# V's blocks of keys 400 instead of 392 bytes apart in SBUF, in an attention kernel with a small expert layer

## The chip, the core and the metric

The kernel runs on one core of a Trainium2 chip. The core has a matrix engine (TensorE, "PE" in the profile; its weight loads are shown apart as "PEld"), VectorE ("DVE"), ScalarE ("ACT"), GpSimd ("POOL") and SyncE ("SP"), and 16 DMA engines. On-chip memory is SBUF, which all engines read, in 128 partitions, and PSUM, into which TensorE writes its products. The metric is the device time of one execution in microseconds (us); lower is better.

## What is computed

The input x is 2048 tokens x 640, in bf16. It is normalised by token (xn). Then two parts follow.

Part A is attention over a cache. There are 32 heads of width 192. The queries are xn @ wq; the keys and values are not computed but taken from a cache, of which only the last 512 keys of each head are used:

```python
q = (x @ wq) per head;  k, v = k_cache[:, :, Sk - 512:], v_cache[:, :, Sk - 512:]
p = softmax(q @ k.T * 192 ** -0.5)
s = concat_heads(p @ v) @ wo
```

Part B picks the two tokens with the highest score x @ w_r, runs a gated layer of width 1536 on them, weighs them with a sigmoid, and adds them to x at their places; a silu follows (g). The output is x + s * g.

## The kernel before

**Tiling.** Heads are worked in pairs: one head sits in partitions 0 to 63, the other in 64 to 127, so most matrix products are issued twice, once for each half r, and the two run side by side in the 64-row halves of TensorE. There are 8 groups of 4 heads (2 pairs a group), and for each group 4 stretches of 512 tokens. A *step* is a group, a stretch and a pair: 64 steps. A *block* b is half a step, 256 tokens: 128 blocks, each with two query tiles a of 128 tokens.

**Stages of a block.** The order on each engine is written out by hand: no scheduler moves anything (`manual_schedule`). From block 12 to 125 one pattern, `BLOCK = "A S0 M0 W m E0 B S1 M1 P E1 l"`, is followed; the blocks before and after have their own lists of tokens (`FIRST`, `LAST`).

- A, B (`q_phase`, L340): the queries of the next step, products with 512 or 256 columns; ScalarE copies them to SBUF (L352).
- S (`scores`, L367): queries times keys, 6 products with 512 columns for each query tile; PSUM has two buffers for them.
- M (`row_max`, L372): VectorE takes the row maxima.
- E (`exps`, L377): ScalarE takes the exponentials. When both tiles of a block are done, SyncE issues a transposing DMA (L383) that turns them into pT.
- P (`o_item`, for block b - 2): the products with V (`o_products`, L406), then the reciprocal of the row sums on VectorE (L413), the scaling into o_sb by VectorE for one head (L417) and by ScalarE for the other (L420), and a transposing DMA (L423) to oT.
- W (`w_item`, for item b - 6): the products with wo (L447), 24 with 320 columns, which VectorE adds to s_acc (L470). It uses the same PSUM banks as P, which must have been read out.
- m, l and the callbacks inside P: pieces of part B, loads for the next group, and the final sums.

**V in SBUF.** V's tile is `v_ring`, [128 partitions, 3 ring places, 8, VC] in bf16, a ring over pairs of heads. Key number 8e + k of a head lies in partition e (plus 64 for the second head) in block k, so k runs from 0 to 7 (`KB` = 8) and each partition holds 8 blocks of 192 values. `VC` is the distance of the blocks in elements. Element 192 of each block is set to 1.0 once at the start by GpSimd (L175); with it the product gives the row sum as its 193rd column. Elements from 193 on are never read or written.

A V load is issued by SyncE for each head (`v_piece`, L136), 32 in all; it writes 8 pieces of 384 bytes in each of 64 partitions. The products that read V are the 32 of a block in L406: for each tile a, for k from 0 to 7, for r in 0 and 1, 193 columns of `v_ring[half(r), ring place, k, 0:193]` move through the array against 128 columns of pT as weights.

v_ring is the last tile of the pool "big". The buffers of pools that are opened later (weights wq and wo, raw, ordered and transposed keys, queries, the first x tiles, part B's tiles) come after it in SBUF.

Of the kernel before, what the change touches and what calls it, by code (L numbers as in the profile page):

```python
# [21 lines left out]
def kernel(ctx, tc, A_x, A_k_cache, A_v_cache, A_wq, A_wo, B_x, B_w_r, B_w_gate, B_w_up, B_w_down, out):  # L22
# [5 lines left out]
    Dh = A_k_cache.shape[3]  # L28
# [49 lines left out]
    xnT = big.tile([P, NTB, DC, P], BF16, name="xnT")  # L78
    s_acc = big.tile([P, NTB, D], FP32, name="s_acc")

    RP, RO, RT, RV, VC = 3, 3, 7, 3, Dh + 4
    p_ring = big.tile([P, 2, 2, KB, 2, HK], BF16, name="pexp")
    pT_ring = big.tile([P, RP, 2, KB, P], BF16, name="pT")
    o_ring = big.tile([P, RO, CC, 2, HK], BF16, name="o_sb")
# [932 lines left out]
```

## Time and profile before

| | |
|---|---|
| median of 3 runs | 795.19 us (794.8 to 796.57) |
| the profiled execution | 796.98 us |
| its span, first to last instruction | 795.1 us |
| granted TensorE clock | 1.000 |
| busy: TensorE / VectorE / ScalarE / GpSimd | 98% / 75% / 66% / 39% |
| products of L406 (V) | 4096 |
| DMA: moved, mean rate | 141.77 MB, 178 GB/s |

Busy times are shares of the span. Matrix products overlap each other and their ends are modelled, so the time that one takes is better read from the starts of successive ones than from the length of one. "Idle before" in a group of instructions is time in which the engine stood still before them, with what ended it. The chain is followed back from the last instruction: at each step to what released it, or to the instruction ahead of it on its engine.

### The profile page before, as it was taken

What the parts mean: (1) busy time and instruction counts of PE and PEld (TensorE: products, weight loads), DVE (VectorE), ACT (ScalarE), POOL (GpSimd) and SP (SyncE); (2) the same over time, 40 slices, a digit from 0 to 9 for tenths busy, and PEclk for the clock granted to TensorE, in tenths of its full rate; (3) what the DMA queues carried; (4) which work ended last, traced back from release to release, by engine and by line L of the source; (5) the groups of instructions that cost most, each with busy time, mean ns of one, the idle gap of its engine ahead of it and who ended that gap; (6) DMA issues with size and microseconds to landing.
All of it is one profiled execution on the core that took longest, in us unless ns stands there. A gap on an engine that the chain in (4) does not pass through costs nothing.

```text
span 795.1 us, 26635 instructions
## 1 busy us (share of the span) xinstructions
PE 779.8 (98%) x11357; PEld 576.6 (73%) x11357; DVE 597.6 (75%) x1091; ACT 525.9 (66%) x952; POOL 313.8 (39%) x248
## 2 busy tenths in 40 slices
PE   8899999999999999999999999999999999999997
PEld 4457677777777677777777777777777777777775
DVE  7898788887778766767766777777777777766775
ACT  6676666666666666666666667767767776666662
POOL 1333111011110101001011499999996412565865
PEclk9999999999999999999999999999999999999999
DMA  9989999799999999999999999999999899999993
GB/s 238 191 174 167 160 192 172 134 195 168 179 204 184 179 196 200 191 181 215 182 213 158 180 189 185 149 163 180 163 188 160 148 188 178 200 174 177 177 176 87
DMA packets 443319, 141.77 MB, mean 178 GB/s; under 512 B 410436, under 2 KB 442696, under 8 KB 443200
## 3 DMA queue, kind: packets, MB, share of 16 engines
q1 hardware_dynamic: 433568, 130.83, 94.6%
q10 hardware_dynamic: 8672, 6.72, 3.5%
q0 software_dynamic: 960, 2.52, 1.2%
q8 instruction: 89, 1.46, 0.8%
q14 instruction: 30, 0.25, 0.1%
HBM read 39.98 MB, written 2.62 MB: 54 GB/s over the span
## 4 chain that ended last, share of the span: by engine, by line
PE 89%; DVE 5%; ACT 3%; DMA 2%; issue 1%; SPq 0%; DVEq 0%; ACTq 0%
PE w L447 25%; PE q_ps L340 23%; PE o_ps L406 20%; PE s L367 19%; DVE nm L372 1%; ACT pexp L377 1%; DMA pT<-pexp 1%; PE q_ps L309 1%; DMA v_sb<-in_A_v_cache_dram 1%; ACT o_sb L420 0%; DVE s_acc L470 0%; ACT xnT L283 0%; DMA x_in<-in_A_x_dram 0%; PE tp L282 0%; PE gu_ps L787 0%
## 5 line engine op out<-in xcount | busy, mean ns | idle before, releaser
L372 DVE TENSOR_REDUCE nm<-s 128x2 f32<-128x1024 f32 x256 | 312.9, 1223 | 120.0 <-PE s L367 114.6
L377 ACT ACTIVATE pexp<-s,nm 128x512 bf16<-128x512 f32 x512 | 323.9, 688 | 103.8 <-DVE nm L372 70.3
L447 PE MATMUL w<-wo_g,oT 64*128 64x320 bf16 x3072 | 231.0, 296 | 2.2 <-ACT o_sb L420 2.1
L340 PE MATMUL q_ps<-xnT,wq_g 64*128 64x512 bf16 (+1 forms) x2340 | 232.4, 323 | 0.3 <-ACT qT L352 0.2
L447 PEld LDWEIGHTS <-oT 64*128 64x128 bf16 x3072 | 170.3, 94 | 60.5 <-issue 2.6
L367 PE MATMUL s<-kT,qT 64*128 64x512 bf16 x1536 | 211.6, 376 | 2.6 <-ACT pexp L377 2.2
L406 PEld LDWEIGHTS <-pT 64*128 64x128 bf16 x4096 | 179.2, 94 | 29.9 <-issue 2.8
L406 PE MATMUL o_ps<-v_sb,pT 64*128 64x193 bf16 x4096 | 197.3, 243 | 1.8 <-DMA v_sb<-in_A_v_cache_dram 0.8
L420 ACT ACTIVATE o_sb<-o_ps,rl 128x192 bf16<-128x192 f32 x250 | 91.7, 418 | 134.8 <-DVE rl L413 129.5
L340 PEld LDWEIGHTS <-wq_g 64*128 64x128 bf16 x2340 | 126.8, 100 | 45.5 <-issue 0.8
L151 POOL COPY wo_g<-wo_g 64x1920 bf16<-64x1920 bf16 x32 | 57.8, 1809 | 216.0 <-DMA wo_g<-in_A_wo_dram 158.5
L367 PEld LDWEIGHTS <-qT 64*128 64x128 bf16 x1536 | 85.0, 94 | 57.5 <-issue 3.5
L470 DVE TENSOR_TENSOR s_acc<-s_acc,w 128x320 f32<-128x320 f32 x192 | 85.0, 484 | 33.7 <-PE w L447 33.7
L352 ACT ACTIVATE qT<-q_ps 128x1024 bf16<-128x1024 f32 x114 | 92.5, 811 | 5.6 <-PE q_ps L340 0.8
L417 DVE TENSOR_TENSOR o_sb<-o_ps,rl 128x384 bf16<-128x384 f32 x131 | 73.1, 558 | 4.5
L121 POOL COPY k_perm<-k_raw 128x768 bf16<-128x768 bf16 x30 | 25.0, 847 | 122.5 <-DMA k_raw<-in_A_k_cache_dram 92.2
L853 POOL TENSOR_SCALAR yh<-y_bc,oh 128x640 bf16<-128x640 bf16 x32 | 61.7, 1927 | 4.8 <-DMA y_bc<-y_d 3.3
L854 POOL TENSOR_TENSOR xn<-xn,yh 128x640 bf16<-128x640 bf16 x32 | 45.2, 1414 | 2.7
L413 DVE RECIPROCAL rl<-o_ps 128x2 f32<-128x2 f32 x256 | 30.5, 160 | 14.5 <-PE o_ps L406 7.6
L918 POOL TENSOR_TENSOR s_acc<-s_acc,x_fin 128x640 f32<-128x640 f32 x16 | 22.4, 1399 | 31.5 <-DMA x_fin<-in_A_x_dram 31.0
L850 POOL TENSOR_SCALAR xn<-xn 128x640 bf16<-128x640 bf16 x16 | 30.0, 1875 | 0.8
L478 POOL TENSOR_TENSOR fin_o<-fin_t,s_acc 128x640 bf16<-128x640 f32 x12 | 18.5, 1541 | 17.6 <-DVE fin_t L473 11.0
(132 smaller groups left out, 264.8 us busy)
## 6 DMA issues: line engine op xcount, KB each, us to landing
wo_g<-in_A_wo_dram SPq DMA_DIRECT2D x32, 240.0 KB, 4.2
k_raw<-in_A_k_cache_dram SPq DMA_DIRECT2D x32, 192.0 KB, 3.4
v_sb<-in_A_v_cache_dram SPq DMA_DIRECT2D x32, 192.0 KB, 4.1
wq_g<-in_A_wq_dram SPq DMA_DIRECT2D x14, 288.0 KB, 3.7
wq_g<-in_A_wq_dram SPq DMA_DIRECT2D x14, 192.0 KB, 3.6
x_fin<-in_A_x_dram SPq DMA_DIRECT2D x16, 160.0 KB, 3.4
pT<-pexp SPq DMA_TRANSPOSE x134, 5.0
oT<-o_sb SPq DMA_TRANSPOSE x126, 3.6
```

The costliest lines, as they stand in the source:

```text
L151: nc.gpsimd.tensor_copy(out=grp[g][("wo", pr)][half(1), cs, :], in_=grp[g][("wo", pr)][half(0), cs, :])
L340: mm = nc.tensor.matmul(q_ps[k][:, 0:n] if type(q_ps) is list else q_ps[:, k, 0:n], lhsT=wq[half(r), dc, c:2 * Dh:3], rhs=xnT[half(r), tok ...
L352: nc.scalar.activation(out=out, in_=q_ps[:, :, 0:n], func=ACT.Copy, scale=scale)
L367: nc.tensor.matmul(s_of[b, a][:, r, :], lhsT=qT_of[i][half(r), c, u * P:(u + 1) * P], rhs=grp[g][("kT", pr)][half(r), :, c, :], start=(c = ...
L372: rm = nc.vector.tensor_reduce(out=nm_of[b, a], in_=s_of[b, a], axis=AX.X, op=ALU.max, negate=True)
L377: nc.scalar.activation(out=p_ring[:, b % 2, a, :, hh, :].rearrange("p (x j) e -> p x j e", x=2), in_=s_of[b, a][:, hh, :].rearrange("p (j ...
L406: nc.tensor.matmul(o_of[b][r][:, a, 0:Dh + 1], lhsT=pT_ring[half(r), b % RP, a, k, :], rhs=v_ring[half(r), (g * PAIRS + pr) % RV, k, 0:Dh ...
L417: nc.vector.tensor_tensor(out=o_sb, in0=src, in1=rl[:, r].unsqueeze(2).unsqueeze(3).to_broadcast([P, 2, 3, HK]), op=ALU.mult)
L420: nc.scalar.activation(out=o_sb[:, a], in_=src[:, a], func=ACT.Copy, scale=rl[:, r, a:a + 1])
L447: nc.tensor.matmul(w_ps[r][:, 0:HD], lhsT=oT_ring[half(r), bs[pr] % RT, c, :], rhs=grp[g][("wo", pr)][half(r), c, cs], start=(pr == 0 and ...
L470: nc.vector.tensor_tensor(out=acc, in0=acc, in1=src, op=ALU.add)
L853: nc.gpsimd.tensor_scalar(out=yh, in0=M["y_bc"][:, j, :], scalar1=M["oh"][:, n, j:j + 1], scalar2=None, op0=ALU.mult)
```

## The change

One number changes: the distance of V's blocks in a partition goes from 196 elements (392 bytes) to 200 (400 bytes). Everything that indexes `v_ring` follows by itself: the loads (L136), the setting of the ones (L175) and the products (L406). Their number, order and sizes stay the same on each engine and queue. v_ring grows from 9408 to 9600 bytes in each partition, and what is placed behind it moves up by 192 bytes.

```diff
-    RP, RO, RT, RV, VC = 3, 3, 7, 3, Dh + 4
+    RP, RO, RT, RV, VC = 3, 3, 7, 3, Dh + 8
     p_ring = big.tile([P, 2, 2, KB, 2, HK], BF16, name="pexp")
     pT_ring = big.tile([P, RP, 2, KB, P], BF16, name="pT")
     o_ring = big.tile([P, RO, CC, 2, HK], BF16, name="o_sb")
     oT_ring = big.tile([P, RT, CC, P], BF16, name="oT")
     v_ring = big.tile([P, RV, KB, VC], BF16, name="v_sb")
```

## The prediction

> **What bounds the kernel now.** I read the page's busy rows first, then its chain of waits, then the list of costly groups, then the timeline of a few steady blocks, and last windows laid over single products.
>
> ```profile
> span 795.1 us, 26635 instructions
> PE 779.8 (98%) x11357; PEld 576.6 (73%) x11357; DVE 597.6 (75%) x1091; ACT 525.9 (66%) x952; POOL 313.8 (39%) x248
> core 0: 795.1 us, clock 1.000
> PE 89%; DVE 5%; ACT 3%; DMA 2%; issue 1%; SPq 0%; DVEq 0%; ACTq 0%
> L406 PE MATMUL o_ps<-v_sb,pT 64*128 64x193 bf16 x4096 | 197.3, 243 | 1.8 <-DMA v_sb<-in_A_v_cache_dram 0.8
> ```
>
> TensorE is busy 98% of the span at full clock and carries 89% of the chain that ended last. V is read by one line only, L406, in 4096 products: 128 blocks x 2 query tiles x 8 keys-in-block k x 2 partition halves. Their engine sat idle for only 1.8 us before them in all. So the question is how long one such product holds TensorE. The mean of 243 ns cannot say, because ends are modelled and products overlap. Starts can. These are consecutive rows of TensorE's timeline (start, length, line, shape, count):
>
> ```profile
> 302.32 1.81 PE L447 MATMUL w<-wo_g,oT 64*128 64x320 bf16 x24
> 303.95 1.26 PE L340 MATMUL q_ps<-xnT,wq_g 64*128 64x512 bf16 x10
> 305.03 0.83 PE L367 MATMUL s<-kT,qT 64*128 64x512 bf16 x6
> 305.68 1.53 PE L406 MATMUL o_ps<-v_sb,pT 64*128 64x193 bf16 x32
> 307.03 0.72 PE L340 MATMUL q_ps<-xnT,wq_g 64*128 64x256 bf16 x10
> 307.57 0.83 PE L367 MATMUL s<-kT,qT 64*128 64x512 bf16 x6
> ```
>
> Products come in pairs, the upper and the lower 64 rows side by side, so I count pairs, from one row's start to the next row's start. 512 columns: (305.03 - 303.95)/5 = 216 ns a pair. 256 columns: (307.57 - 307.03)/5 = 108 ns. 320 columns: (303.95 - 302.32)/12 = 135.8 ns. That is 0.422 ns a column with almost nothing on top, and by it 193 columns should take 81.4 ns. The sixteen V pairs take (307.03 - 305.68)/16 = 84.4 ns, 3 ns more than their columns explain.
>
> The diff says where to look. A block of V starts 392 bytes after the one before it, and 392 = 24.5 x 16. The built program puts v_ring at byte 135,328 of each partition, which is 8458 x 16, in both kernels. So the blocks with even k begin on a multiple of 16 bytes today, those with odd k 8 bytes past one. The trace of before therefore already holds both cases side by side. I laid windows over the first query tile of 21 steady blocks, each from the start of the first product of one k to the start of the first product of the next k: 84 windows for even k (first and last window, then the sum) and 84 for odd k. The columns are the window, its length, the busy time of V's products and of their weight loads in it, the granted clock and the DMAs' share and rate.
>
> ```profile
> 274.69:274.78 0.08, 0.08 (x2) 0.08 (x2) 1.00 1.29 290
> ...
> 415.31:415.39 0.08, 0.08 (x7) 0.08 (x4) 1.00 1.07 237
> sum 6.95, PE 6.95 PEld 6.91; mean PE 0.08 PEld 0.08
> ...
> 274.78:274.86 0.09, 0.09 (x4) 0.09 (x4) 1.00 1.85 410
> ...
> 415.39:415.48 0.09, 0.09 (x7) 0.09 (x4) 1.00 1.27 289
> sum 7.26, PE 7.26 PEld 7.26; mean PE 0.09 PEld 0.09
> ```
>
> Even k: 6.95/84 = 82.7 ns a pair. Odd k: 7.26/84 = 86.4 ns. The even ones lie near the line of the other products (81.4), the odd ones 5 ns above it. The difference is (7.26 - 6.95)/84 = 3.7 ns a pair.
>
> **The change part by part.** No instruction is added, removed or moved on any engine or queue, so nothing is passed over and no wait is new. What changes are addresses.
>
> *The reads of V.* After it all k begin on a multiple of 16 (400 = 25 x 16). Pairs with odd k: 128 blocks x 2 tiles x 4 = 1024. At the even price the gain is 1024 x 3.7 ns = 3.8 us of TensorE time, 0.030 us a block. The bounds: nothing, if the offset isn't what makes odd k long, and 1024 x (86.4 - 81.4) = 5.1 us if the pairs fell to the line itself. I take the even pairs' price, since they are the same instruction on the same tile.
>
> [...]
>
> *How much of it reaches the end.* The blocks run TensorE without a gap, so a shorter V stage pulls all that follows forward, unless something else sets the next start. The chain names other engines for 11% of the span: at the ends, and around the few blocks with routing work. Taking that as the share in which the gain is swallowed, 0.89 x 3.8 = 3.4 us are left. This is an estimate from the chain's shares; its ends are 3.8 (nothing swallowed) and 1.9 (next paragraph).
>
> Who is late next? In every other block the w stage starts just when the evacuation of o is done:
>
> ```profile
> 402.99 1.53 PE L406 MATMUL o_ps<-v_sb,pT 64*128 64x193 bf16 x32
> 403.28 1.22 DVE L372 TENSOR_REDUCE nm<-s 128x2 f32<-128x1024 f32 x1 [0.94 <-PE s L367]
> 404.56 0.24 DVE L413 RECIPROCAL rl<-o_ps 128x2 f32<-128x2 f32 x2
> 404.88 0.83 PE L367 MATMUL s<-kT,qT 64*128 64x512 bf16 x6
> 405.08 0.41 ACT L420 ACTIVATE o_sb<-o_ps,rl 128x192 bf16<-128x192 f32 x1
> 405.55 0.45 PE L447 MATMUL w<-wo_g,oT 64*128 64x320 bf16 x4
> ```
>
> The last o_sb ends at 405.08 + 0.41 = 405.49, w starts 0.06 us later, and the scores before it needed TensorE until about 404.88 + 3 x 0.216 = 405.53. So w waits for a chain that begins with the reciprocal at 404.56. That one follows the end of o (402.99 + 1.53 = 404.52), and VectorE's row maximum ends at 403.28 + 1.22 = 404.50. With o 0.030 us shorter, o ends at 404.49 and the reciprocal can follow; VectorE is free 0.06 us before today's start. So w moves forward with o, but with only about 0.03 us to spare: the row maximum is late next.
>
> *The loads of V and the ones column.* 32 loads write the same 384-byte pieces, 400 bytes apart; the one memset of the ones column (L175) writes as many elements, long before the first product.
>
> ```profile
> DMA v_sb<-in_A_v_cache_dram: 1.7, 2
> DMA pT<-pexp: 1.3, 3
> DMA to landing us min/median/max: 3.3/4.1/5.7
> 35.55 1.18 PE L406 MATMUL o_ps<-v_sb,pT 64*128 64x193 bf16 x24 [0.77 <-DMA v_sb<-in_A_v_cache_dram]
> L175 POOL MEMSET v_sb<- x1: 195/195/195, 1.6 to 1.6; 128x24 bf16 x1
> L406 PE MATMUL o_ps<-v_sb,pT x4096: 240/243/254, 23.1 to 782.2; 64*128 64x193 bf16 x196
> ```
>
> The third row is for the V loads, the first two are all that the V stage's engines (weight loads included) ever waited for DMAs. A load at the slow end instead of the median would be 1.6 us later; exposed is only the V stage at 35.55 us, which waits for one now, so the bounds are +1.6 and -0.8 us (the wait on TensorE gone), and I take 0, as the byte count and piece count stay. Without that cover, all 32 loads 1.6 us later would cost 51 us, but each is issued blocks ahead.
>
> *Everything placed after v_ring* (wq, wo, k, kT, qT buffers) moves by 3 x 8 x 8 = 192 bytes, a multiple of 16, 32 and 64, so matrix operands keep their place within such lines. For the DMAs, these rows show the cover of pT:
>
> ```profile
> 401.36 2.10 SPq L383 DMA_TRANSPOSE pT<-pexp  x1
> DMA to landing us min/median/max: 3.4/5.0/6.9
> ...
> 92.63 1.65 PE w L447 x24
> 104.44 1.64 PE w L447 x24
> ```
>
> The second row is pT's landing; the last two, from the chain in order of time, show that two blocks repeat in 11.81 us, so one takes 5.91. The pT issued at 401.36 is used one block after the V stage at 402.99, at about 408.9, 7.5 us later; it lands in 5.0. So 2.5 us are to spare in the median and 0.6 at worst; blocks that come 0.030 us sooner do not use that up. I take 0; the bounds are the 1.3 us waited for pT now, gone or doubled.
>
> **Sum.** Profiled execution: 796.98 us, of which 795.1 are span. Minus 3.4 gives 793.6. The median of the three runs is 795.19, 1.8 below the profiled execution; on it the forecast is 795.19 - 3.4 = 791.8 us, 0.43% faster. A measurement of this kernel can tell about 0.2%, 1.6 us.
>
> **The rivals.**
>
> *Half the gain* (chance 0.09). If the reciprocal cannot move up because of the row maximum before it, w in every other block starts where it does now, and only 64 blocks gain: 64 x 0.030 = 1.9 us, 793.3 us. For it speaks the margin of 0.03 us, against it that 0.06 us were free.
>
> *Nothing* (0.13). Odd k could be long for something else that alternates with k, or the pairs could be paced at 84.4 ns on the average by their weight loads, with the alternation only the rhythm in between. Then 795.2 us. [...] For the weight loads speaks that they fill the windows as fully as the products do (6.91 of 6.95); against it, that the even pairs sit near the line of columns, which a mere average has no reason to do.
>
> *Slower* (0.07). The windows run from start to start, so the 3.7 ns could belong to the product that comes next: a product that begins on a multiple of 16 would pay for it. The point that decides is which of the two offsets pays. If it is the aligned one, all pairs become long ones and the kernel loses what I expect it to gain, 1024 x 3.7 = 3.8 us: 799.0 us. Against it: the operands of q, s and w all begin on multiples of 16 and keep to 0.422 ns a column without such an extra.
>
> **How the numbers follow.** Forecast 0.71 (own range 791.0 to 792.4), half 0.09, nothing 0.13, slower 0.07. Faster by over 0.2% is forecast and half: 0.80; same 0.13; slower 0.07. The range goes from 795.19 - 3.8 - 0.8 = 790.6, the full gain and the early wait gone too, up to 794.8, past the half gain and to the edge of nothing; some of nothing and all of slower are left out.
>
> **What would show it.** Laid over the changed kernel, windows for odd k should sum to what those for even k do, about 6.95 for 84. In the timeline the V stage should take 1.32 instead of 1.35 us from its start to the next stage's. Two blocks should repeat in 11.75 us instead of 11.81. The w stage should still start 0.06 us after the last o_sb; if it starts later than the s stage lets it, half the gain is gone there. I am wrong if odd pairs stay at 86 ns, if even pairs rise to it, or if waits of the V stage for pT grow.

## The result and the profile after

The changed kernel takes 795.17 us (median of 22 runs, 794.09 to 798.0); 22 runs of the kernel before beside it have a median of 796.94. The ratio is 0.9976, with a 95% interval of 0.9964 to 0.9987: faster by 0.24%, 1.0 to 2.9 us. The forecast was a gain of 3.4 us (0.43%) and a time of 791.8, in a range from 790.6 to 794.8. The sign was right, the size twice too large, and the time lies above the range. The three runs that the forecast started from lay at 795.19, 1.75 us below the median of the 22: of the 3.4 us by which the time missed the forecast, 1.75 come from that start and 1.6 from the gain.

The page of the profile after, by busy time, by the chain, and for V's products:

```profile
span 792.6 us, 26635 instructions
PE 778.2 (98%) x11357; PEld 576.8 (73%) x11357; DVE 594.5 (75%) x1091; ACT 526.1 (66%) x952; POOL 313.8 (40%) x248
PE 89%; DMA 4%; DVE 3%; ACT 2%; issue 1%; SPq 0%; ACTq 0%; DVEq 0%
L406 PE MATMUL o_ps<-v_sb,pT 64*128 64x193 bf16 x4096 | 195.6, 243 | 3.0 <-DMA pT<-pexp 1.6 <-DMA v_sb<-in_A_v_cache_dram 0.8 <-DVE xnT L283 0.6
```

TensorE bounds the kernel as before, and V's products fill 1.7 us less of the span (197.3 before). Now the windows of the prediction, laid in the same way over the changed kernel: first and last window and the sum for the 84 even k, then for the 84 odd k.

```profile
273.55:273.63 0.08, 0.08 (x2) 0.08 (x2) 1.00 1.18 265
...
414.01:414.10 0.08, 0.08 (x7) 0.08 (x4) 1.00 0.07 20
sum 7.00, PE 7.00 PEld 6.96; mean PE 0.08 PEld 0.08
...
273.63:273.71 0.08, 0.08 (x4) 0.08 (x4) 1.00 1.20 272
...
414.10:414.18 0.08, 0.08 (x7) 0.08 (x4) 1.00 0.06 15
sum 7.00, PE 7.00 PEld 7.00; mean PE 0.08 PEld 0.08
```

The alternation is gone, but both kinds stand at 7.00/84 = 83.3 ns. Odd k fell from 86.4 to 83.3; even k *rose* from 82.7 to 83.3. So part of what odd k had cost before was given back by the even k beside it.

From here on I use one window for the eight pairs of the first query tile of a block, 21 blocks, in which a rhythm within the tile adds up. Before, then after:

```profile
274.69:275.37 0.68, 0.68 (x16) 0.68 (x16) 1.00 2.90 242
...
sum 14.20, PE 14.20 PEld 14.17; mean PE 0.68 PEld 0.67
```

```profile
273.55:274.21 0.67, 0.67 (x16) 0.67 (x16) 1.00 1.54 195
...
sum 14.00, PE 14.00 PEld 13.97; mean PE 0.67 PEld 0.67
```

A pair takes 14.20/168 = 84.5 ns before and 14.00/168 = 83.3 after. Does the saving arrive? The w stage of every second block in the chain, over four periods of two blocks, before and after:

```profile
92.63 1.65 PE w L447 x24
...
139.85 1.64 PE w L447 x24
```

```profile
92.47 1.64 PE w L447 x24
...
139.58 1.64 PE w L447 x24
```

47.22 us before, 47.11 after: 14 ns a block, and 128 x 14 ns = 1.8 us. That is the measured gain. From 21 blocks in the middle, the windows give (14.20 - 14.00)/21 = 9.5 ns a tile, at most 19 a block. So three quarters of the saving or more arrive; there was only less of it than forecast.

### The profile page after: what moved, and what is told of

Read it like the earlier page. It is cut to its first block, busy times and chain, and to the rows that moved or that the text cites. A ratio compares the mean times of both kernels' runs of the same rounds, so it can differ in the third digit from the quotient of the medians.

```text
span 792.6 us, 26635 instructions
## 1 busy us (share of the span) xinstructions
PE 778.2 (98%) x11357; PEld 576.8 (73%) x11357; DVE 594.5 (75%) x1091; ACT 526.1 (66%) x952; POOL 313.8 (40%) x248
## 4 chain that ended last, share of the span: by engine, by line
PE 89%; DMA 4%; DVE 3%; ACT 2%; issue 1%; SPq 0%; ACTq 0%; DVEq 0%
PE w L447 25%; PE q_ps L340 23%; PE o_ps L406 20%; PE s L367 19%; DMA pT<-pexp 4%; ACT pexp L377 1%; PE q_ps L309 1%; DVE nm L372 1%; DMA v_sb<-in_A_v_cache_dram 1%; ACT xnT L283 0%; DMA x_in<-in_A_x_dram 0%; PE tp L282 0%; PE gu_ps L787 0%; DVE fin_t L473 0%; DVE fin_o L475 0%
## 5 line engine op out<-in xcount | busy, mean ns | idle before, releaser
L406 PEld LDWEIGHTS <-pT 64*128 64x128 bf16 x4096 | 177.6, 94 | 31.2 <-issue 2.8
L406 PE MATMUL o_ps<-v_sb,pT 64*128 64x193 bf16 x4096 | 195.6, 243 | 3.0 <-DMA pT<-pexp 1.6
```

Of the source, the lines that this page charges most:

```text
L406: nc.tensor.matmul(o_of[b][r][:, a, 0:Dh + 1], lhsT=pT_ring[half(r), b % RP, a, k, :], rhs=v_ring[half(r), (g * PAIRS + pr) % RV, k, 0:Dh ...
```

## The experiments

Three theories were put to the test. A: an offset of 8 bytes has a price of its own, as the prediction had it. B: it is the switch of the offset from one product to the next that costs. Neither held, and C, formed on the way, says that it costs when a product *begins in the same 16 bytes of SBUF in which the product before it ended*. At 392 bytes the block of an even k ends with byte 385 after its start, and the next begins at byte 392: both lie in bytes 384 to 399. An odd k ends at byte 777 and the next block begins at 784, which is in the next 16 bytes. So four of a tile's eight products began in shared 16 bytes before. At 400 bytes none does. The distance alone can't be it: in both cases at 392 bytes, 6 bytes lie between the end and the next start. For each run the first of its 21 tile windows and their sum are shown.

**All blocks 8 bytes off, 400 bytes apart.**

```diff
-    v_ring = big.tile([P, RV, KB, VC], BF16, name="v_sb")
+    v_flat = big.tile([P, RV * KB * VC + 16], BF16, name="v_sb")
+    v_ring = v_flat[:, 4:4 + RV * KB * VC].rearrange("p (v k c) -> p v k c", v=RV, k=KB)
```

> The blocks of V stay 400 bytes apart as in the changed kernel, but all of them begin 8 bytes past a multiple of 16 (data starts at element 4 of the ring). Windows of the changed kernel: odd k 7.00/84 = 83.3 ns a pair, even k 83.3; before 86.4 and 82.7, mean 84.6. Theory A, the offset has a price of its own: a product that begins 8 bytes past a line is 2 x (84.6 - 83.3) = 2.5 ns longer in steady state, whoever its neighbours are, and before the even ones got 0.6 of it back. Then every pair takes about 85.8 to 86.4 ns, 128 x 16 x 2.5 = 5.1 us more than the changed kernel: about 800 us, ratio to before about 1.003. Theory B, the switch: what costs is that successive products begin at different offsets. Then all pairs take about 83.3 ns, and the time is the changed kernel's, ratio about 0.998.

Measured: ratio to before 0.9981 (0.9961 to 1.0), the changed kernel's time as near as this can tell.

```profile
273.38:274.04 0.67, 0.67 (x16) 0.67 (x16) 1.00 1.11 221
...
sum 14.01, PE 14.01 PEld 13.98; mean PE 0.67 PEld 0.67
```

14.01/168 = 83.4 ns a pair with no block on a multiple of 16. The offset has no price: theory A falls, and with it the stated purpose of the change. What the change did that mattered was something else.

**Blocks packed, 386 bytes apart.**

```diff
-    RP, RO, RT, RV, VC = 3, 3, 7, 3, Dh + 8
+    RP, RO, RT, RV, VC = 3, 3, 7, 3, Dh + 1
```

> The blocks of V lie 386 bytes apart, with no padding: block k begins 2k bytes past a multiple of 16, so one run shows all eight even byte offsets. Theory A with a price for any offset but 0: k = 0 about 83 ns, the seven others about 86; the mean 85.6, 128 x 16 x (85.6 - 84.6) = 2 us slower than before, ratio about 1.0026. Theory A with a price only where the first line holds 4 values or fewer (8 bytes or more past): k = 0 to 3 about 83, k = 4 to 7 about 86, the mean as before, ratio about 1.000. Theory B, the switch: every product switches its offset, all pairs near 86, ratio about 1.004.

Measured: ratio 1.0051 (1.0026 to 1.0075), slower than before.

```profile
275.19:275.87 0.69, 0.69 (x16) 0.69 (x16) 1.00 1.57 188
...
sum 14.43, PE 14.43 PEld 14.40; mean PE 0.69 PEld 0.69
```

14.43/168 = 85.9 ns. At the time this seemed to speak for a switch at each step. By theory C seven of eight steps share 16 bytes here (each block starts where the last one ended): (14.43 - 14.00)/(21 x 7) = 2.9 ns each. Half of the blocks also begin at an odd element, which has a small price of its own, 0.9 ns (below); without it 2.4 ns a step are left.

**208 columns, blocks 416 bytes apart.**

```diff
-    RP, RO, RT, RV, VC = 3, 3, 7, 3, Dh + 8
+    RP, RO, RT, RV, VC = 3, 3, 7, 3, Dh + 16
...
-    nc.gpsimd.memset(v_ring[:, :, :, Dh:Dh + 1], 1.0)
+    nc.gpsimd.memset(v_ring[:, :, :, Dh:VC], 1.0)
...
-                                     rhs=v_ring[half(r), (g * PAIRS + pr) % RV, k, 0:Dh + 1],
+                                     rhs=v_ring[half(r), (g * PAIRS + pr) % RV, k, 0:208],
```

The products write 208 columns too; the ones fill elements 192 to 207 of each block.

> V's blocks 416 bytes apart, each beginning on a multiple of 32 bytes, and the products with V take 208 columns instead of 193 (the extra columns are constant ones and are not read back). This asks what paces an aligned pair. If its columns do, 15 columns at 0.422 ns make it 83.3 + 6.3 = 89.6 ns, and the time grows over the changed kernel by 128 x 16 x 6.3 ns = 13 us, to about 808 us, ratio to before 1.014. If the weight loads do, a pair stays at about 83.3 ns and the ratio at about 0.998; anything between says both.

Measured: ratio 1.0088 (1.0054 to 1.0122).

```profile
276.99:277.70 0.71, 0.71 (x16) 0.71 (x16) 1.00 0.98 106
...
sum 14.99, PE 14.99 PEld 14.95; mean PE 0.71 PEld 0.71
```

14.99/168 = 89.2 ns: 15 columns more cost 5.9 ns, 0.39 ns each. A pair is paced by its columns and not by its weight loads. The ratio falls short of the 1.014 expected by columns: 2048 x 5.9 ns are 12 us, and about 9 of them show (1.0088 against the changed kernel's 0.9976). It is not 0.422 ns a column with nothing on top, either. The prediction's rows for 320 and 512 columns give (216 - 135.8)/192 = 0.418 ns a column and 2.1 ns on top. An estimate by that line is 89.0 ns for 208 columns, against 89.2 measured, and 82.7 for 193, against 83.3. So the 81.4 ns, drawn without the 2.1, was no mark that a pair could reach by alignment.

**Only the tiles behind v_ring moved.** The kernel before, with an unused tile of 192 bytes:

```diff
     v_ring = big.tile([P, RV, KB, VC], BF16, name="v_sb")
+    big.tile([P, 96], BF16, name="pad")
```

> V's blocks stay 392 bytes apart and offset as before; an unused tile of 192 bytes is put behind v_ring, so that everything placed after it moves up as in the changed kernel. If the gain comes from the reads of V alone, the pairs stay at 82.7 and 86.4 ns and the ratio is 1.000. If moving the other tiles did part of it, up to 1.9 us of it shows here, ratio down to 0.9976.

Measured: ratio 1.0004 (0.9985 to 1.0023).

```profile
274.79:275.47 0.68, 0.68 (x16) 0.68 (x16) 1.00 1.41 216
...
sum 14.20, PE 14.20 PEld 14.17; mean PE 0.68 PEld 0.67
```

The pairs are those of before. The move of the other tiles did nothing to them, and nothing to the time outside the interval, which goes from 1.2 us less to 1.8 us more.

**The order of k alone.** The kernel before, no address moved:

```diff
-            for k in range(KB):
+            for n, k in enumerate((0, 2, 4, 6, 1, 3, 5, 7)):
...
-                                     start=(k == 0), stop=(k == KB - 1))
+                                     start=(n == 0), stop=(n == KB - 1))
```

> The kernel before, blocks 392 bytes apart, with only the order of the products changed: k = 0, 2, 4, 6, 1, 3, 5, 7 instead of 0 to 7. The same 16 odd and even pairs are computed in each block, but the offset changes twice in eight pairs instead of eight times. Theory B, the switch (the constant offset of 8 bytes cost nothing): pairs of about 83.3 ns, with one long and one short interval in each eight; the mean of a tile's pairs 83.3 + 2.0/8 = 83.6, two blocks in about 11.78 us instead of 11.81, ratio about 0.998, though no address has moved. Theory A, a price of the product's own offset: the sum is that of before, mean 84.3 ns, ratio 1.000.

Measured: ratio 0.9975 (0.9957 to 0.9994), the gain of the change without the change. Its tile windows, and after them the windows of its fourth pair (k = 6, followed by 1) and of its fifth (k = 1, followed by 3):

```profile
273.27:273.94 0.67, 0.67 (x16) 0.67 (x16) 1.00 1.52 224
...
sum 14.01, PE 14.01 PEld 13.98; mean PE 0.67 PEld 0.67
...
sum 1.75, PE 1.75 PEld 1.75; mean PE 0.08 PEld 0.08
...
sum 1.80, PE 1.80 PEld 1.80; mean PE 0.09 PEld 0.09
```

The sum is that of a kernel with no bad step at all: 14.01. There is still a longer interval after the first odd k, 1.80/21 = 85.7 ns, but the pairs behind it make up for it. A long interval alone is thus no cost; only the sum over a tile is. This also hits theory B, which wanted two paid switches a tile (83.6 ns, a sum of 14.04); the next two runs decide against it.

**Alternating offsets without shared bytes, blocks 408 bytes apart.**

```diff
-    RP, RO, RT, RV, VC = 3, 3, 7, 3, Dh + 8
+    RP, RO, RT, RV, VC = 3, 3, 7, 3, Dh + 12
```

> Blocks 408 bytes apart (25.5 x 16): even k on a multiple of 16, odd k 8 bytes past, as before, but a block no longer begins in the 16 bytes in which the block before it ends (392 + 0 lies in the same 16 bytes as byte 385; 408 does not). Theory B, the switch of the offset: 82.5 and 86.1 ns by turns, as before, mean 84.3. Theory C, two successive products sharing 16 bytes of SBUF: all pairs 83.3.

This kernel and those below have one execution each (794.28, 796.36, 801.06, 795.43, 796.02, 808.73 and 794.38 us, in the order shown), so their intervals between products are compared and not their times. The offset switches by 8 bytes at every step, as before. The tile windows, and then those of k = 1 and of k = 3 alone:

```profile
273.69:274.35 0.67, 0.67 (x16) 0.67 (x16) 1.00 1.19 198
...
sum 14.03, PE 14.03 PEld 13.99; mean PE 0.67 PEld 0.67
...
sum 1.80, PE 1.80 PEld 1.80; mean PE 0.09 PEld 0.09
...
sum 1.73, PE 1.73 PEld 1.73; mean PE 0.08 PEld 0.08
```

14.03/168 = 83.5 ns, the sum that theory C asks for; theory B wanted 84.3. That all pairs would be equal, as I wrote for C, is wrong: k = 1 shows 1.80/21 = 85.7 ns and k = 3 shows 82.4. A rhythm with almost no net cost again: 0.03 us over 21 tiles are 1.4 ns a tile, where the change saved 9.5.

**One half of the array at offset 0, the other at 8.**

```diff
+    v_half = [v_flat[:, o:o + RV * KB * VC].rearrange("p (v k c) -> p v k c", v=RV, k=KB) for o in (0, 4)]
...
-                                     rhs=v_ring[half(r), (g * PAIRS + pr) % RV, k, 0:Dh + 1],
+                                     rhs=v_half[r][half(r), (g * PAIRS + pr) % RV, k, 0:Dh + 1],
```

The loads and the ones go by the same two views.

> Blocks 400 bytes apart; the half in partitions 0 to 63 begins on multiples of 16, the half in partitions 64 to 127 always 8 bytes past. Each half of the array sees one offset, but successive products alternate. Theory B for the whole engine: each product switches, so a pair has two switches instead of one and costs at least the 84.3 ns of before, perhaps 85.3. Theory B for each half by itself: 83.3 ns.

```profile
274.79:275.46 0.67, 0.67 (x16) 0.67 (x16) 1.00 1.16 187
...
sum 14.01, PE 14.01 PEld 13.98; mean PE 0.67 PEld 0.67
```

83.4 ns. A switch between successive products of the two halves costs nothing that shows beside the 83.3 of the changed kernel; theory B for the whole engine falls.

**All blocks 2 bytes off, and all 4 bytes off, 400 bytes apart.** As the first experiment, with the data starting at element 1 or at element 2 of the ring.

> Blocks 400 bytes apart, all beginning 2 bytes past a multiple of 16, an address that is not even a multiple of 4. Theory B: 83.3 ns a pair, span near that of the changed kernel, 792.6. A price of the odd element itself: 85.7 ns, as the pairs of the packed layout take, two blocks 11.85 us.

> Blocks 400 bytes apart, all 4 bytes past a multiple of 16. With all at 2 bytes past, a pair took 84.2 ns instead of 83.3, with nothing shared. If that price belongs to addresses that are not a multiple of 4 bytes, it is gone here: 83.3 ns. If it belongs to any small offset, it stays: 84.2.

Tile windows for 2 bytes, with the landing of its V loads, then the same for 4 bytes:

```profile
276.80:277.47 0.67, 0.67 (x16) 0.67 (x16) 1.00 1.36 203
...
sum 14.15, PE 14.15 PEld 14.12; mean PE 0.67 PEld 0.67
...
DMA to landing us min/median/max: 4.2/5.2/8.0
```

```profile
273.07:273.73 0.67, 0.67 (x16) 0.67 (x16) 1.00 1.17 192
...
sum 14.03, PE 14.03 PEld 13.99; mean PE 0.67 PEld 0.67
...
DMA to landing us min/median/max: 3.3/4.2/5.7
```

At 2 bytes a pair takes 84.2 ns, 0.9 more, and the loads of V land in 5.2 us instead of 4.1; at 4 bytes (83.5 ns, 4.2 us) nothing is left of either. So the price goes with the odd element, in TensorE's reads and, as it seems, in the DMA's writes; 2 bytes is the only such start tried by itself. V's loads landed in 4.1 us before and after the change, in 4.3 with all blocks 8 bytes off, and in 4.6 in the packed run, where half of the blocks begin at an odd element. The span at 2 bytes was 799.3 us in its one execution, 6.7 more than the changed kernel's; 2048 x 0.9 ns are 1.8 of that. TensorE also stood idle before V's products for 5.5 us in all instead of 3.0, mostly for DMAs; the rest is open.

**The offsets of before exchanged: 392 bytes apart, starting 8 bytes in.** The view of the first experiment at a distance of `Dh + 4`.

> Blocks 392 bytes apart as before, but the ring's data begins 8 bytes in: even k lie 8 bytes past a multiple of 16, odd k on one. Theory C (it costs about 2 ns when a product begins in the same 16 bytes in which the product before it ended): now the ends of k = 1, 3, 5 share their last 16 bytes with the starts of k = 2, 4, 6; k = 0 shares with nothing. Long intervals after the starts of k = 2, 4, 6, three in eight; mean of a tile's pairs 83.3 + 3 x 2/8 = 84.1, two blocks about 11.80 us. Theory A, a price of the offset of 8 bytes: long at k = 0, 2, 4, 6, mean 84.3, two blocks 11.81.

Tile windows, then the windows of k = 0 alone and of k = 2 alone:

```profile
274.49:275.16 0.67, 0.67 (x16) 0.67 (x16) 1.00 1.18 217
...
sum 14.15, PE 14.15 PEld 14.12; mean PE 0.67 PEld 0.67
...
sum 1.75, PE 1.75 PEld 1.72; mean PE 0.08 PEld 0.08
...
sum 1.84, PE 1.84 PEld 1.84; mean PE 0.09 PEld 0.09
```

k = 0 and k = 2 have the same offset. k = 2 begins where k = 1 ended and takes 1.84/21 = 87.6 ns; k = 0 begins apart from everything and takes 83.3. The sum, 84.2 ns a pair, is that of three steps and not of four: (14.15 - 14.00)/(21 x 3) = 2.4 ns for each, and before (14.20 - 14.00)/(21 x 4) = 2.4.

**Shared 16 bytes with everything aligned.** Blocks 400 bytes apart; the products read 208 columns, on into the next block (which k = 7, with 200 columns, does not). The ones fill elements 192 to 199 of each block.

```diff
+    v_rows = v_ring.rearrange("p v k c -> p v (k c)")
...
+    n = 208 if k < KB - 1 else VC
-    nc.tensor.matmul(o_of[b][r][:, a, 0:Dh + 1], ..., rhs=v_ring[half(r), ..., k, 0:Dh + 1], ...)
+    nc.tensor.matmul(o_of[b][r][:, a, 0:n], ..., rhs=v_rows[half(r), ..., k * VC:k * VC + n], ...)
```

> Blocks 400 bytes apart, all on multiples of 16, but the products of k = 0 to 6 take 208 columns and so read on into the first 16 bytes of the next block (k = 7 takes 200; the extra columns are not read back). No offset changes anywhere; only the shared 16 bytes are new against the kernel with 208 columns and 416 bytes, whose pairs take 89.2 ns. Theory C: seven of eight pairs gain about 2 ns; mean over the eight (7 x 89.2 + 86.0 + 14)/8 = 90.5. Without a price for sharing: 88.8.

```profile
278.36:279.09 0.73, 0.73 (x16) 0.73 (x16) 1.00 1.62 189
...
sum 15.33, PE 15.33 PEld 15.29; mean PE 0.73 PEld 0.73
```

15.33/168 = 91.2 ns, against 89.2 with 208 columns and nothing shared. By columns alone the sum would be 14.99 less 21 x 8 x 0.39 ns = 14.92. The rest, 0.41 us over 21 x 7 steps, is 2.8 ns for each step that begins in 16 bytes just read, a little more than the 2 that the expectation used. No block has an offset here, so this is the suspected cost by itself.

**Falling order.** The kernel before, k from 7 to 0.

```diff
-            for k in range(KB):
+            for k in reversed(range(KB)):
...
-                                     start=(k == 0), stop=(k == KB - 1))
+                                     start=(k == KB - 1), stop=(k == 0))
```

> The kernel before with the products in falling order, k = 7 to 0. The offsets alternate by 8 bytes at every step as before, but no product begins where its forerunner ended: its own last 16 bytes were the first ones of the forerunner, 80 ns earlier. Theory C: mean 83.3 ns, two blocks 11.78 us. Theories A and B (offset, or its switch): mean 84.3, 11.81.

```profile
273.66:274.33 0.67, 0.67 (x16) 0.67 (x16) 1.00 1.42 235
...
sum 14.04, PE 14.04 PEld 14.01; mean PE 0.67 PEld 0.67
```

14.04/168 = 83.6 ns, next to 83.3, with the addresses and offsets of before. The same 16 bytes are read by neighbours, but as the last of the later product and the first of the earlier one. Only end-then-start costs: of the 9.5 ns that a tile of before paid, at most 0.04 us/21 = 1.9 are left.

No run made a kernel that is shown to beat the changed one; the reordered one equals it, as near as its interval can tell, without any padding.

## Where the prediction was right and where it failed

*What bounds the kernel, and where to look.* Right. TensorE bounds the steady blocks, the even and odd k of before are two cases side by side, and their sum has something to give.

*The price of an aligned pair.* This is the step that failed: "At the even price the gain is 1024 x 3.7 ns = 3.8 us", with the reason that the even pairs are the same instruction on the same tile. They were the same instruction but not in the same company. An interval from start to start contains what the neighbour before left behind: the even k of before were 0.6 ns quicker than a pair that follows an undisturbed one. The two kinds had to be added up, not compared. Their mean was 84.5 ns, and the right price was 83.3, which no row of before showed. TensorE thus had 2048 x 1.2 ns = 2.4 us to gain and not 3.8, and two blocks repeat in 47.11/4 = 11.78 us, where the prediction wanted 11.75. That the even pairs lay near the line of 81.4 ns had no weight: the line left out the 2.1 ns on top of the columns that the rows for 320 and 512 columns give.

*The cause.* Wrong, and the forecast's sign was right for another reason, which is luck. The multiple of 16 does nothing by itself (the run 8 bytes off keeps the gain with 83.4 ns a pair; the exchanged one pays for three steps with 84.2, before paid for four with 84.5). The wider distance moved the start of each odd block out of the 16 bytes in which its forerunner ended.

*The share that arrives.* Not settled. 14 ns of at most 19 a block are a share of 0.74 or more, and 1.8 us of 2.4 are 0.75, with an interval (1.0 to 2.9 us) in which 0.89 lies too. That the engines at the ends and around the routing work swallow the rest was not tested.

*The late chain in every other block.* Right, in the same stage of the changed kernel:

```profile
401.73 1.52 PE L406 MATMUL o_ps<-v_sb,pT 64*128 64x193 bf16 x32
402.02 1.23 DVE L372 TENSOR_REDUCE nm<-s 128x2 f32<-128x1024 f32 x1 [0.94 <-PE s L367]
403.29 0.24 DVE L413 RECIPROCAL rl<-o_ps 128x2 f32<-128x2 f32 x2
404.27 1.81 PE L447 MATMUL w<-wo_g,oT 64*128 64x320 bf16 x24
```

The reciprocal came 1.56 us after the start of o (1.57 before) and w 2.54 (2.56 before); the row maximum, over at 403.25, did not hold it up. But o ended at 401.73 + 1.52 = 403.25 too, so in this block no margin is left. The rival of half the gain has the right size and the wrong mechanism.

*Nothing, and slower.* Part of the alternation was indeed a rhythm, as the rival of nothing had it, but not for the weight loads: 15 more columns cost 5.9 ns a pair. That the aligned product pays is refuted by the 83.3 ns of all.

*Loads, the other tiles.* Right in the landings: the loads of V land in 4.1 us and those of pT in 4.8, as the first two of these rows of the changed kernel show, and the run with the tiles moved alone gave 1.0004.

```profile
DMA to landing us min/median/max: 3.3/4.1/6.0
...
DMA to landing us min/median/max: 3.1/4.8/7.2
...
DMA pT<-pexp: 3.9, 4
```

Not in the waits. The last row says that the V stage waited for pT for 3.9 us in all, weight loads included, against 1.3 before: more than the doubling that the prediction allowed for, and one of its own signs of being wrong. For the products without their weight loads the wait was 0.4 us before and 1.6 after, the latter all in one wait; it was 1.1 and 0.8 with all blocks 8 and 4 bytes off, and 1.1 in the packed run. So, with one execution of each, it is not shown that the change made it longer.

## What to carry to other kernels

Where products that follow each other overlap, the price of one of two alternating kinds can't be read from its own interval: add up a whole period, and compare periods. An address change has more effects than its name says; before "alignment" is believed, run one kernel that keeps everything but the alignment, and one that reorders without moving an address. When TensorE walks through adjacent short rows, let a product not begin in the 16 bytes in which the last one ended, which cost 2.4 to 2.8 ns a step here: pad the row, or change the order.

## What was not expected of the hardware

A product that begins in the 16 bytes of SBUF in which the product before it on the same partitions ended held TensorE 2.4 ns longer (before, exchanged), 2.8 ns with everything aligned. At 400 bytes an even block ends and the next one begins within the same 32 bytes (384 to 415), and odd and even k took the same 83.3 ns there; bytes 385 and 392 of before share 16 bytes but no 8, so of 8, 16 and 32 bytes these runs leave 16. An offset of 4 or 8 bytes cost nothing that shows in a product (83.5 and 83.4 ns against 83.3); 2 bytes cost 0.9 ns a pair, and the DMAs to such addresses landed in 5.2 instead of 4.1 us in the one execution. What in the reading path causes it, and why some offsets make a rhythm of 82.4 and 85.7 ns with almost no cost in the sum, these runs do not show.
